# First product of blocks 3 to 6 with seven multiplications for eight, in a fused attention and feed-forward kernel

## The chip, the cores and the metric

The kernel runs on one core of one Trainium2 chip. The metric is device microseconds for one launch; lower is better. Three runs of the kernel before took 614.77, 615.26 and 616.49 us; the median is 615.26.

## The reference

Chunked attention with a few memory keys, and after it two matrix products with a gate between them:

```python
for c in range(nc):                          # 24 chunks of 32 queries, 4 x 8 heads of 64
    k_ctx = k[:, :, l_start:r_end]           # 16 keys to the left, 8 to the right
    k_full = np.concatenate([mem_k, k_ctx], axis=2)     # 8 memory keys ahead
    v_full = np.concatenate([mem_v, v_ctx], axis=2)
    scores = scale * np.matmul(q_c, k_full.transpose(0, 1, 3, 2))
    a = softmax(scores)
    out[:, :, c_start:c_end] = np.matmul(a, v_full)
x = out.transpose(0, 2, 1, 3).reshape(3072, 512)
h = x @ w_in                                 # 512 x 2048, the first product
g = np.where(h >= 1, h, np.where(h <= -1, 0.0, (h + 1) ** 2 / 4))
return g @ w_out                             # 2048 x 512, the second product
```

All of it is in float32.

## The kernel before, in words

The 3072 tokens are cut into six blocks of 512 (`TB`); the text counts them from 1, the code from 0. For each block, attention yields x transposed, with 512 features in four slices of 128 partitions (`NP`) by 512 tokens. The hidden width of 2048 is cut into 16 slices of 128 (`NFC`), and one slice of one block is a step.

Every float32 operand of the two products is split into two float32r parts, a high one (the rounded value) and a low one (the rest), and each product is made of three: high by high, high by low, low by high. `pe_hidden` (line 398) so has 12 matmuls a step, 4 slices of features by 3, with 128x128 weights as the stationary and 512 tokens as the moving operand, into one PSUM bank `ps_h`. `gating` (407) makes the gate on ScalarE from two Relus that read the bank and a Square; `gate_sum` (417) joins them on VectorE, `gate_high` (422) rounds on ScalarE to `gh`, and `gate_low` (428) subtracts on VectorE to `gl`. `pe_out` (433) has 12 matmuls of 512 columns, 4 groups of 128 tokens by 3, with gh and gl as stationary, accumulated over all 16 steps into four banks `ps_o`. A step is thus 24 matmuls of 512 columns, and `pe_out` follows two steps (`LAG`) after `pe_hidden`.

The weights come as 64-bit words, 16 tiles of 1 MB (`load_w`), and `decode` (153) turns each in place into high and low parts `wr`, with five VectorE and two ScalarE instructions, four of the seven on 128x1024 words. They stay in SBUF, so they are decoded while block 1 runs.

Blocks 1 and 2 are worked in half steps of 256 tokens (`half_step`, 452): 12 matmuls of 256 columns into `ps_h`, the gate on 256 columns, 6 matmuls of 512 columns. In the table `FIRST` (32) the letters A and B are the halves of block 1, C and D of block 2, w a decode, g attention of block 1, n0 to n3 the attention halves of blocks 2 and 3, and + the next load. A name stands once for each stage of its chain, and the table sets the order in which all engines get their instructions. From block 3 on, the loop at line 590 sets the order, a step at a time, with the attention of the next block begun at steps 3 and 9 (`STARTS`).

The attention of a half block (`attention`, 374, or the same calls in the loop) is `pe_scores` (64 matmuls of 64 columns, `ps_s`; the trace shows each float32 matmul of the attention twice), `less_max` (two VectorE instructions of 128x1024), an Exp on ScalarE, `normalise` (four on VectorE), `transpose_prob` (six VectorE transposes), `pe_values` (`ps_x`), `x_high` (two ScalarE copies out of PSUM) and `x_low` (two VectorE subtractions). Each half's qk and v tiles are loaded ahead from SyncE's queue, into one buffer each.

All engines' instructions are kept in program order (`InOrder`, 60), so no engine takes a later instruction while an earlier one waits. SyncE issues all loads and stores but the last half store. All these calls go through line 68, the line that the profile shows for them; the tiles' names tell them apart.

Of the kernel before, what the change touches and what calls it, by code (L numbers as in the profile page):

```python
# [27 lines left out]
FIRST = """
    + + g0 g0 g0 + g0 g1 g0 + g0 g0 g1 g1 g0 g1 + g1 g0 w0 g1 g1 + g1 g0 w0 g1 w0 + g0 g1 w0 w0 g2 +
    g0 w0 g1 w1 g2 + g2 g1 g0 g3 g2 + g1 g2 A0 + g3 g3 g2 g2 g3 g2 A1 A0 + g3 w2 g3 g3 g3 g2 w1 A1
    w1 + g2 g3 w3 w1 g2 g3 A0 w1 g3 w2 + w2 g2 g3 A0 g2 w4 g3 A0 B0 w1 + w2 A0 B0 A1 w2 B0 B1 w3 +
    B0 w2 A1 A2 B1 B0 A1 w3 A1 + A2 B1 w5 w3 B0 B1 A2 w3 + B1 B2 w4 A2 w3 w6 B1 A2 B2 + w4 A3 w7 B2
    w4 B2 A2 A3 + B2 w5 w4 B3 A3 w5 w8 B2 A3 w4 + B3 A4 w9 A3 B3 w5 B3 A3 + A4 B3 w6 w5 A4 B4 w6 A4
    w10 + A4 B3 w5 B4 A5 w11 w6 + B4 w6 A4 w7 w7 B4 A5 B5 B4 w12 + A5 w6 B4 A5 B5 A5 w7 w13 A6 + B5
    w7 w8 A5 w8 B5 A6 B6 B5 w14 A6 w7 A6 B5 B6 A6 w8 w15 A7 B6 w8 w9 A6 w9 B6 A7 B6 B7 A7 w8 A7 B6
    B7 A7 w9 A8 B7 w9 w10 w10 A7 B7 A8 B7 B8 A8 w9 A8 B7 A8 B8 w10 A9 B8 w10 w11 w11 B8 A8 A9 B8 A9  # L40
    B9 w10 A9 A9 B8 w11 B9 B9 A10 w11 w12 w12 B9 A9 A10 B9 w11 B10 A10 w12 A10 B9 B10 A10 w12 w13
    A11 B10 w13 B10 A10 A11 B10 w12 n0 A11 w13 A11 B11 + n0 w13 B10 A11 B11 n0 A12 B11 n0 w13 B11
    A11 A12 n0 B12 n0 n0 B11 n0 B11 B12 A12 n0 A12 A13 A12 n0 n0 A12 A13 w14 n0 B13 w14 n0 A14 B13
    n0 B12 n0 w14 B12 B12 w14 A13 w15 B12 A13 + w14 n0 A13 A14 B14 w15 A13 n0 n0 B14 B13 n1 w15 B13
    B13 w15 A15 A14 + n1 A14 B13 A15 A14 w15 B15 n1 A14 B14 n1 A15 B14 n1 C0 A15 B15 n1 n1 B14 n1
    B14 C0 A15 n1 A15 n1 n1 C1 n1 n1 C2 C1 B15 n1 B15 C0 B15 n1 C0 A15 C2 C0 C1 A15 C2 C1 C2 B15 C1
    + n1 C2 n1 n1 C0 B15 D0 B15 C1 D0 D0 D1 D0 D0 C3 D1 D1 C2 D1 C3 D1 D0 C3 C3 C3 D2 D1 D2 D2 D3 D2
    D2 C4 D3 D3 C3 D3 C4 D3 D2 C4 C4 C4 D4 D3 D4 D4 D5 D4 D4 C5 D5 D5 C4 D5 C5 D5 D4 C5 C5 C5 D6 D5
# [671 lines left out]
```

## Time and profile before

| | |
|---|---|
| Median of three runs | 615.26 us (614.77 to 616.49) |
| Span of the profiled execution | 613.5 us; its own time is not listed apart, and the median is 1.8 us above the span |
| TensorE matmul busy | 596.3 us, 97% |
| TensorE weight load busy | 500.1 us, 82% |
| VectorE busy | 331.1 us, 54% |
| ScalarE busy | 291.3 us, 47% |
| Mean granted TensorE clock | 0.983 |
| DMA | 55.36 MB, 90 GB/s over the span |

PE stands for TensorE's matmuls, PEld for its weight loads, DVE for VectorE, ACT for ScalarE, SP for SyncE. Matmuls are pipelined: the record of one reaches past the start of the next, so the distance from start to start is what one costs in a stream. A row of a group gives the instruction with what it writes and reads, the count, the busy time, the mean ns of one, and how long the engine had been idle before it. A row of the chain gives start, length, engine, the tile written and the count.

### The profile page before, as it was taken

How to read it: one execution, taken by the hardware profiler on the slowest of the kernel's cores; microseconds unless marked ns; L12 is line 12 of the kernel's file. 1: busy time of each engine (PE TensorE's matmuls, PEld its weight loads, DVE VectorE, ACT ScalarE, POOL GpSimd, SP SyncE). 2: the span in 40 equal slices, each digit the busy share in tenths (PEclk: the TensorE clock that was granted, in tenths of full speed). 3: DMA queues.
4: the chain of work that ended last, by engine and by line, in shares of the span. 5: the costliest groups of instructions: out<-in, count | busy, mean ns of one | idle time of the engine just before them, and what ended most of it. 6: DMA issues, size and time to landing. Idle time of an engine off the chain costs nothing.

```text
span 613.5 us, 12988 instructions
## 1 busy us (share of the span) xinstructions
PE 596.3 (97%) x5784; PEld 500.1 (82%) x5784; DVE 331.1 (54%) x514; ACT 291.3 (47%) x599; POOL 0.7 (0%) x6
## 2 busy tenths in 40 slices
PE   5899999999999999999999999999999999999997
PEld 2789998889988888888888888888888888888885
DVE  5899999983266734735523643732563732322222
ACT  2689865554444454434344344344443434433442
POOL 0000000000000000000000000000000000000000
PEclk7689999999999999999999999999999999999999
DMA  9999002322022222122201212100410000100001
GB/s 356 423 417 411 7 1 105 131 93 90 0 105 88 87 71 92 81 71 104 71 0 70 104 70 105 38 33 0 173 69 2 0 2 0 70 0 2 0 1 68
DMA packets 9992, 55.36 MB, mean 90 GB/s; under 512 B 1104, under 2 KB 1360, under 8 KB 5328
## 3 DMA queue, kind: packets, MB, share of 16 engines
q1 hardware_dynamic: 9792, 54.40, 23.1%
q8 instruction: 45, 0.74, 0.5%
q10 hardware_dynamic: 144, 0.13, 0.1%
q14 instruction: 11, 0.09, 0.1%
HBM read 48.23 MB, written 6.29 MB: 89 GB/s over the span
## 4 chain that ended last, share of the span: by engine, by line
PE 79%; DVE 16%; issue 2%; ACT 1%; DMA 1%
PE ps_h L68 37%; PE ps_o L68 37%; DVE f L68 5%; PE ps_x L68 3%; PE ps_s L68 2%; DVE wr L68 2%; DVE gw L68 2%; DVE pr L68 1%; DVE gl L68 1%; DVE pt L68 1%; DVE den L68 1%; DVE mx L68 1%; DMA qk<-in_first_qk_dram 1%; DVE xtl L68 1%; ACT pr L68 0%
## 5 line engine op out<-in xcount | busy, mean ns | idle before, releaser
L68 PE MATMUL ps_h<-xth,wr 128*128 128x256 f32 (+1 forms) x1024 | 273.3, 341 | 0.3 <-ACT xth L68 0.3
L68 PE MATMUL ps_o<-wr,gh 128*128 128x512 f32 x768 | 241.6, 396 | 0.0
L68 PEld LDWEIGHTS ps_h<-xth,wr 128*128 128x128 f32 x1024 | 180.9, 192 | 24.4 <-ACT xth L68 0.4
L68 PE MATMUL ps_h<-xtl,wr 128*128 128x256 f32 (+1 forms) x512 | 166.1, 340 | 1.0 <-DVE xtl L68 1.0
L68 PEld LDWEIGHTS ps_o<-wr,gh 128*128 128x128 f32 x768 | 141.7, 189 | 29.4
L68 DVE SCALAR_TENSOR_TENSOR gw<-gw,gt 128x256 f32<-128x256 f32 (+1 forms) x128 | 71.1, 557 | 168.3 <-ACT gw L68 167.5
L68 PE MATMUL ps_o<-wr,gl 128*128 128x512 f32 x384 | 151.6, 395 | 0.1
L68 ACT ACTIVATE gw<-ps_h 128x256 f32<-128x256 f32 (+1 forms) x128 | 62.6, 489 | 166.8 <-PE ps_h L68 165.8
L68 PEld LDWEIGHTS ps_h<-xtl,wr 128*128 128x128 f32 x512 | 98.2, 192 | 14.0 <-DVE xtl L68 1.6
L68 DVE TENSOR_TENSOR gl<-gw,gh 128x256 fp32r<-128x256 f32 (+1 forms) x128 | 70.8, 555 | 66.5 <-ACT gh L68 65.7
L68 ACT CAST gh<-gw 128x256 fp32r<-128x256 f32 (+1 forms) x128 | 65.5, 514 | 63.9 <-DVE gw L68 63.9
L68 PEld LDWEIGHTS ps_o<-wr,gl 128*128 128x128 f32 x384 | 72.4, 189 | 18.1 <-DVE gl L68 1.1
L68 ACT ACTIVATE gw<-gw 128x256 f32<-128x256 f32 (+1 forms) x128 | 67.3, 526 | 0.0
L68 ACT ACTIVATE gt<-ps_h 128x256 f32<-128x256 f32 (+1 forms) x128 | 62.2, 486 | 0.0
L68 DVE STREAM_TRANSPOSE pt<-pr 32x512 f32<-32x512 f32 (+1 forms) x60 | 41.2, 698 | 1.3
L68 DVE SCALAR_TENSOR_TENSOR f<-w,f 128x1024 uint32<-128x1024 uint32 x32 | 39.1, 1221 | 0.4
L68 ACT ACTIVATE pr<-pr 128x1024 f32<-128x1024 f32 (+1 forms) x14 | 13.1, 938 | 41.2 <-DVE pr L68 41.2
L68 PEld LDWEIGHTS ps_x<-pt,v 64*64 64x64 f32 x1536 | 25.6, 142 | 5.4 <-issue 3.4
L68 PE MATMUL ps_x<-pt,v 64*64 64x32 f32 x1536 | 27.4, 226 | 1.1 <-DVE pt L68 0.6
L68 ACT CAST xth<-ps_x 128x512 fp32r<-128x512 f32 x24 | 13.0, 594 | 24.8 <-PE ps_x L68 24.8
L68 PEld LDWEIGHTS ps_s<-qk 64*32 64x32 f32 x1536 | 16.9, 110 | 8.0 <-issue 4.6
L68 PE MATMUL ps_s<-qk 64*32 64x64 f32 x1536 | 19.5, 235 | 3.3 <-issue 1.4
(27 smaller groups left out, 179.3 us busy)
## 6 DMA issues: line engine op xcount, KB each, us to landing
w<-in_w_dram SPq DMA_DIRECT2D x16, 1024.0 KB, 19.7
qk<-in_qk_dram SPq DMA_DIRECT2D x10, 1536.0 KB, 6.5
v<-in_vw_dram SPq DMA_DIRECT2D x10, 1024.0 KB, 4.9
out_dram<-ob SPq DMA_DIRECT2D x23, 256.0 KB, 2.0
qk<-in_first_qk_dram SPq DMA_DIRECT2D x4, 768.0 KB, 8.7
v<-in_first_v_dram SPq DMA_DIRECT2D x4, 512.0 KB, 12.7
out_dram<-ob ACTq DMA_DIRECT2D x1, 128.0 KB, 2.3
out_dram<-ob SPq DMA_DIRECT2D x1, 128.0 KB, 2.5
```

Source lines behind the costliest of these rows:

```text
L68: return self.tc.keep_in_program_order(getattr(self.engine, name)(*args, **kwargs))
```

## The change

Blocks 3 to 6 make the first product in another way. Four slices of the hidden width form a quad, two pairs `s` of slices. For each pair the product of 512 features by 256 hidden columns with 512 tokens is cut in halves on all three sides, and made with Winograd's form of Strassen's scheme: seven products instead of eight, of sums of weights (four for each pair, in `build`) and of sums of x (`S1` to `S4`, in `SUMS`). A product has two times 6 matmuls of 256 columns (2 slices of features by 3), one half bank for each pair. The products add up in place in two banks, X and Y. Of h's four quarters, 11, 12 and 22 are made from a ScalarE copy of X (`copy_out`) to which VectorE adds Y (`add_up`); 21 is read in X. Gate, rounding and second product then go on as before, in groups of 12 second-product matmuls (`pe_out`), with the same number in all.

The sums of weights are made in block 2, in eight builds (the letter t in `FIRST`): two VectorE adds of a weight's high and low parts, four subtractions, one ScalarE cast to the high part, one VectorE subtraction for the low part, into the one buffer `st`, from which a 1 MB store goes to DRAM (`saved`). From there they are read back for each quad into holes, the places of weights in SBUF that blocks 3 to 6 no longer need: two loads of 256 KB after each of four products (`load_t`). Blocks 4 and 6 go through the quads in reverse, so that the quad at a turn is not loaded anew.

The attention of blocks 3 to 6 leaves x in plain float32 (`x_plain`, two ScalarE copies a half); `sum_up` (four VectorE instructions a block) and `split` (seven pairs of a ScalarE rounding and a VectorE subtraction) take the place of the four low parts. The order of blocks 3 to 6 is no longer set by a loop over steps but by the tables `QUADS`, one for each quad of a block: p is a product, c a copy out, a the adding up, r the Relus and Square, m the joining, h and l the high and low parts, g a group of second products, d a sum and k a split of x, 0 and 1 the next stage of an attention half of the next block, @S and @V its scores and values with the next loads, z a store; a leading minus means the quad before. x's tiles of blocks 1 and 2 have pools of their own, which are given up to the new tiles; gh and gl have four buffers instead of three, and the identity takes one of gl's until it is needed.

```diff
-LAG = 2
-STARTS = (3, 9)
+SECOND = 2
 FIRST = """
...
-    + n1 C2 n1 n1 C0 B15 D0 B15 C1 D0 D0 D1 D0 D0 C3 D1 D1 C2 D1 C3 D1 D0 C3 C3 C3 D2 D1 D2 D2 D3 D2
...
+    C1 + n1 C2 n1 n1 C0 B15 t0 C1 D0 B15 D0 t0 D0 D1 t0 D0 t0 C3 t0 C2 D0 D1 t0 t0 D1 t0 C3 t1 C3
...
+PROD = {
+    1: ("X", "A11", None),
+    2: ("Y", "A12", None),
+    6: ("X", "S2", 0),
+    5: ("Y", "S1", 1),
+    7: ("X", "S3", 2),
+    4: ("X", "A22", 3),
+    3: ("Y", "S4", None),
+}
+QUADS = (
...
+    p1 -h12 1 p2 c1 1 a11 r11 1 -l12 m11 -g21 -g22 p6 1 c2 p5 1 p7 c3 a22 h11 -g12 r22 m22 l11 1 p4
...
-    ident = const.tile([P, P], F32, name="ident")
+    ident = gpool.tile([P, P], F32, name="ident", tag="gl", bufs=4)
...
-        x_high(key)
-        yield
-        yield from x_low(key)
+        if key[0] < SECOND:
+            x_high(key)
+            yield
+            yield from x_low(key)
+        else:
+            x_plain(key)
+            yield
...
+    saved = dram.tile([NFC // 2, P, 4, 2, HQ], F32, name="saved")
+    def build(m):
...
+        fef = apool.tile([P, 2, 2, HQ], F32, name="fef", tag="f", bufs=2)
+        for j in range(2):
+            hi, lo = (weights(0, 2 * m + j, part).bitcast(F32) for part in range(2))
+            dve.tensor_tensor(fef[:, j].rearrange("p a b -> p (a b)"), hi, lo, op=ALU.add)
+            yield
+        b11, b21, b12, b22 = (fef[:, j, k] for j in range(2) for k in range(2))
+        tf = apool.tile([P, 4, HQ], F32, name="tf", tag="f", bufs=2)
+        dve.tensor_tensor(tf[:, 1], b12, b11, op=ALU.subtract)
+        yield
+        dve.tensor_tensor(tf[:, 2], b22, b12, op=ALU.subtract)
+        yield
+        dve.tensor_tensor(tf[:, 0], b22, tf[:, 1], op=ALU.subtract)
+        yield
+        dve.tensor_tensor(tf[:, 3], b21, tf[:, 0], op=ALU.subtract)
+        yield
+        st = ahead["y0"].tile([P, 4, 2, HQ], F32R, name="st", tag="st")
+        act.copy(st[:, :, 0], tf)
+        yield
+        dve.tensor_tensor(st[:, :, 1], tf, st[:, :, 0].bitcast(F32), op=ALU.subtract)
+        sp.dma_start(saved[m], st.bitcast(F32))
+        yield
+    def load_t(i, q):
+        for s in range(2):
+            sp.dma_start(hole(i, s).bitcast(F32), saved[2 * q + s, :, i])
...
+    def split(name):
+        k = side(name)
+        src = plain_of(name) if name != "S3" else plain["s"][:, 1]
+        act.copy(k[:, 0], src)
+        dve.tensor_tensor(k[:, 1], src, k[:, 0].bitcast(F32), op=ALU.subtract)
...
+    def product(i, q):
+        to, name, _ = PROD[i]
+        x = side(name)
+        for s in range(2):
+            terms = [(0, 0, cc) if lo == 0 else (0, 1, cc) for cc in range(2) for lo in range(2)]
+            terms += [(1, 0, cc) for cc in range(2)]
+            for n, (wp, xp, cc) in enumerate(terms):
+                pe.matmul(
+                    bank[to][:, s * HQ : (s + 1) * HQ],
+                    stationary(i, q, s, wp)[:, cc * P : (cc + 1) * P],
+                    x[:, xp, cc],
+                    start=i in (1, 2, 5) and s == 0 and n == 0,
...
+    def copy_out(n, key):
...
+        act.copy(t, bank["X"])
...
+    def add_up(name, key):
+        h = now.pop((*key, {"11": "c1", "22": "c3", "12": "c2"}[name]))
+        dve.tensor_tensor(h, h, bank["Y"], op=ALU.add)
...
+            elif what == "p":
+                i = int(which)
+                product(i, q)
+                if PROD[i][2] is not None and at + 1 < len(line) and line[at + 1][1] != q:
+                    load_t(PROD[i][2], line[at + 1][1])
```

Where the orders differ: first TensorE in the middle of block 3, before. `ps_h` with `xth` and `xtl` is a step's first product, `ps_o` with `gh` and `gl` the second; the numbers are those of the tiles.

```order
1516 L68 MATMUL ps_o_3946<-wr_12_1167,gh_4589 128x512 x2
1517 L68 MATMUL ps_o_3946<-wr_12_1167,gl_4590 128x512
1518 L68 MATMUL ps_o_3946<-wr_12_1167,gh_4589 128x512 x2
1519 L68 MATMUL ps_o_3946<-wr_12_1167,gl_4590 128x512
1520 L68 MATMUL ps_h_4665<-xth_3327,wr_13_1289 128x512 [waits Activation_49]
1521 L68 MATMUL ps_h_4665<-xtl_3328,wr_13_1289 128x512
```

And now, in the third quad of block 3: products 6, 5 and 7 (`s2`, `s1` and `s3` are the sums of x), `ps_h_3094` being bank X and `ps_h_3095` bank Y, with the waits for the read-back (DMAHW).

```order
1081 L94 MATMUL ps_h_3094<-s2_2962,wr_0_247 128x256 [waits DMAHW3_49,Activation_49]
1082 L94 MATMUL ps_h_3094<-s2_2962,wr_0_247 128x256 x5
1083 L94 MATMUL ps_h_3094<-s2_2962,wr_2_556 128x256 [waits DMAHW4_49]
1084 L94 MATMUL ps_h_3094<-s2_2962,wr_2_556 128x256 x5
1085 L94 MATMUL ps_h_3095<-s1_3085,wr_4_696 128x256 [waits DMAHW5_49,DVE_49]
1086 L94 MATMUL ps_h_3095<-s1_3085,wr_4_696 128x256 x5
1087 L94 MATMUL ps_h_3095<-s1_3085,wr_6_813 128x256 [waits DMAHW6_49]
1088 L94 MATMUL ps_h_3095<-s1_3085,wr_6_813 128x256 x5
1089 L94 MATMUL ps_h_3094<-s3_3088,wr_8_943 128x256 [waits DMAHW7_49,Activation_49]
1090 L94 MATMUL ps_h_3094<-s3_3088,wr_8_943 128x256 x5
```

In place of 12 wide matmuls into a bank of the step's own, 12 narrow ones each go to X, Y and X again, and row 1089 waits for ScalarE's copy of what 1081 to 1084 added up.

That copy on ScalarE, before (one step's gate and the rounding of the next):

```order
487 L68 ACTIVATE gw_5129<-ps_h_5116 128x512 [waits PE_49]
488 L68 ACTIVATE gt_5130<-ps_h_5116 128x512
489 L68 ACTIVATE gw_5129<-gw_5129 128x512 [waits Activation_49]
490 L68 CAST gh_5147<-gw_5129 128x512 [waits DVE_49]
491 L68 ACTIVATE gw_5164<-ps_h_5151 128x512 [waits PE_49]
```

And now, in the quad before the one above (`gt` and `u2` take the copies of X, `gh` is the rounding, `xp` the plain x of the next block's attention):

```order
350 L94 COPY gt_3390<-ps_h_3094 128x512 [waits PE_49]
351 L94 ACTIVATE gw_3409<-gt_3390 128x512 [waits DVE_49]
352 L94 ACTIVATE gt_3390<-gt_3390 128x512 [waits Activation_49]
353 L94 ACTIVATE gw_3409<-gw_3409 128x512
354 L94 COPY u2_3440<-ps_h_3094 128x512 [waits PE_49]
355 L94 CAST gh_3442<-gw_3409 128x512 [waits DVE_49]
356 L94 COPY gt_3542<-ps_h_3094 128x512 [waits PE_49]
357 L94 ACTIVATE gw_3545<-gt_3542 128x512 [waits DVE_49]
```

The gate no longer reads the bank but a copy to which VectorE has added Y, and the second copy (354) stands behind the three gating operations of the first (351 to 353).

Last VectorE early in block 2, before: only the joining (`gw`) and the low part (`gl`) of half steps.

```order
205 L68 SCALAR_TENSOR_TENSOR gw_2020<-gw_2020,gt_2021 128x256 [waits Activation_49]
206 L68 TENSOR_TENSOR gl_2023<-gw_2020,gh_2022 128x256 [waits PE_49,Activation_49]
207 L68 SCALAR_TENSOR_TENSOR gw_2020<-gw_2020,gt_2021 128x256 [waits Activation_49]
208 L68 TENSOR_TENSOR gl_2023<-gw_2020,gh_2022 128x256 [waits Activation_49]
209 L68 SCALAR_TENSOR_TENSOR gw_2088<-gw_2088,gt_2089 128x256 [waits Activation_49]
```

And now, with the second build (`fef` the whole weights, `tf` their sums, `st` the parts to be stored):

```order
205 L94 TENSOR_TENSOR fef_1964<-wr_1_477 128x512
206 L94 SCALAR_TENSOR_TENSOR gw_1948<-gw_1948,gt_1949 128x256 [waits Activation_49]
207 L94 TENSOR_TENSOR fef_1964<-wr_2_556 128x512
208 L94 TENSOR_TENSOR tf_1990<-fef_1964 128x256 [waits DVE_49]
209 L94 TENSOR_TENSOR tf_1990<-fef_1964 128x256
210 L94 TENSOR_TENSOR gl_1951<-gw_1948,gh_1950 128x256 [waits Activation_49]
211 L94 TENSOR_TENSOR gl_1951<-gw_1948,gh_1950 128x256
212 L94 SCALAR_TENSOR_TENSOR gw_2008<-gw_2008,gt_2009 128x256 [waits Activation_49]
213 L94 TENSOR_TENSOR tf_1990<-fef_1964,tf_1990 128x256 [waits DVE_49] x2
214 L94 TENSOR_TENSOR fef_2021<-wr_3_625 128x512 [waits DVE_49]
215 L94 TENSOR_TENSOR gl_2011<-gw_2008,gh_2010 128x256 [waits Activation_49]
216 L94 TENSOR_TENSOR st_2019<-tf_1990,st_2019 128x4x256 [waits DMAHW2_49,Activation_49]
```

Between the gating of half steps stand the builds' instructions, each ahead of gating that comes later in the order.

More of the change, by code (lines that the diff above doesn't have):

```diff
@@ L179, in x_of @@
         if blk not in xts:
[L180 removed]
+            xts[blk] = [xpools[blk].tile([P, NP, TB], F32R, name=n) for n in ("xth", "xtl")]
         return xts[blk]
@@ new lines, in attn_ffn_kernel, with pe_out @@
+    HOUT = {"11": (0, 0), "12": (1, 0), "21": (0, 1), "22": (1, 1)}
+    begun = set()
+    def pe_out(blk, q, name, pieces=None):
+        odd, half = HOUT[name]
+        gh, gl = now[blk, q, name, "g"]
+        if blk not in acc:
+            acc[blk] = [None] * NT
+        if acc[blk][2 * half] is None:
+            pair = two_banks(f"a{half}", "ps_o")
+            acc[blk][2 * half : 2 * half + 2] = [pair[:, t] for t in range(2)]
+        for s, t in pieces or ((0, 0), (0, 1), (1, 0), (1, 1)):
+            fc = 2 * (2 * q + s) + odd
+            wh, wl = weights(1, fc, 0), weights(1, fc, 1)
+            ts = slice(s * HQ + t * P, s * HQ + (t + 1) * P)
+            to = (blk, 2 * half + t)
+            for i, (g, w) in enumerate(((gh, wh), (gh, wl), (gl, wh))):
+                pe.matmul(
+                    acc[blk][2 * half + t], g[:, ts], w, start=to not in begun, stop=True, skip_group_check=True
+                )
+                begun.add(to)
@@ new lines, in attn_ffn_kernel, with small @@
+    order = {}
+    for blk in range(SECOND, NB):
+        order[blk] = list(range(NQ))[:: 1 if blk % 2 == 0 else -1]
+    line = [(blk, q) for blk in range(SECOND, NB) for q in order[blk]]
+    def small(shape, name, tag, bufs, dtype=F32):
+        return gpool.tile(shape, dtype, name=name, tag=tag, bufs=bufs)
+    def copy_out(n, key):
+        if n == 2:
+            t = small([P, TB], "u2", "u2", 1)
+        else:
+            t = small([P, TB], "gt", "gt", 2)
+        act.copy(t, bank["X"])
+        now[(*key, f"c{n}")] = t
@@ new lines, in left, with left_store, finish @@
+    def left(which):
+        two = {"22": (0, 2), "21": (2, 4), "12": (4, 4)}[which]
+        for blk, half, fc in items[len(items) - LAST :][slice(*two)]:
+            next(chains[f"{'ABCD'[2 * blk + half]}{fc}"], None)
+    def left_store(half):
+        for _ in chains["CD"[half] + str(NFC - 1)]:
+            pass
+    def finish():
+        key = line[-1]
+        high("12", key)
+        low("12", key)
+        for t in range(2):
+            pe_out(*key, "22", ((0, t), (1, t)))
+            pe_out(*key, "21", ((0, t), (1, t)))
+            last_store(2 + t)
+        for t in range(2):
+            pe_out(*key, "12", ((0, t), (1, t)))
+            last_store(t)
+        let_go("y0")
+        let_go("y1")
```

387 lines of the change are left out of this document (232 added, 155 removed).

## The prediction

> **What bounds the kernel now.** I read the busy times first, then the slices of the span, then the chain that ended last in order of time, then TensorE's waits.
>
> ```profile
> PE 596.3 (97%) x5784; PEld 500.1 (82%) x5784; DVE 331.1 (54%) x514; ACT 291.3 (47%) x599; POOL 0.7 (0%) x6
> ...
> PE   5899999999999999999999999999999999999997
> ...
> DVE  5899999983266734735523643732563732322222
> ACT  2689865554444454434344344344443434433442
> ```
>
> TensorE is busy in every slice but the first, second and last. VectorE is full only up to about 125 us (the eighth slice ends at 123 us), where the weights are decoded; after that it stands between 2 and 7 tenths. So what happens to TensorE's own work decides, unless new waits appear. The chain in order of time gives TensorE's pace, first in block 2 (half steps, 256 columns a matmul), then in blocks 3 to 6 (full steps, 512 columns):
>
> ```profile
> 155.35 1.43 PE ps_h L68 x12
> 156.79 1.39 PE ps_o L68 x6
> 158.17 2.87 PE ps_h L68 x24
> 161.05 2.77 PE ps_o L68 x12
> ...
> 241.89 1.41 PE ps_s L68 x91
> ...
> 536.80 2.76 PE ps_h L68 x12
> 539.56 2.80 PE ps_o L68 x12
> ...
> 597.89 2.76 PE ps_h L68 x12
> 600.65 8.38 PE ps_o L68 x36
> ```
>
> From 536.80 to 597.89 lie 11 full steps: 61.09 / 11 = 5.554 us for 24 matmuls, 0.2314 us each. In block 2, 24 matmuls of 256 columns take 2.87 us, 0.1196 us each. That is a little more than half of 0.2314 (0.1157), so a narrow matmul pays about 4 ns of its own. Before the steady part, TensorE hardly waits, even while VectorE is full:
>
> ```profile
> PE ps_x L68 <- DVE pt L68: 0.6, 2, 0.4
> PE ps_h L68 <- DVE xtl L68: 0.5, 1, 0.5
> PE ps_s L68 <- issue: 0.4, 1, 0.4
> ```
>
> These are all of TensorE's waits between 60 and 250 us, 1.5 us together. The profiled span is 613.5 us. The runs have a median of 615.26, which leaves 1.8 us around the span; I add these at the end.
>
> **The products.** Before, four steps held 4 x 12 matmuls of 512 columns for the first product and as many for the second: 4 x 5.554 = 22.22 us. A quad replaces them. Its first product has 7 products x 12 matmuls of 256 columns, 84 x 0.1196 = 10.05 us, and its second product is unchanged, 48 x 0.2314 = 11.11 us, together 21.16. That is 1.06 us less a quad. There are 16 quads: **17.0 us less TensorE work**, all of it on the path. If second-product matmuls are priced at 2.80 for 12, as they stand beside 512-column work, the gain is 16 x (4 x 2.76 - 10.05) = 15.8; if at 2.77, as they stand beside 256-column work, 16 x (22.22 - 10.05 - 11.08) = 17.4. I keep 15.8 to 17.4 as its bounds and take 17.0, the pace averaged over both kinds. One eighth of the first product would have been 22 us (16 x 11.04 / 8); the rest goes to the narrower matmuls.
>
> Narrower matmuls also mean 336 weight loads a block for 192, and a row shows what a load takes by itself:
>
> ```profile
> L68 PEld LDWEIGHTS ps_h<-xth,wr 128*128 128x128 f32 x1024 | 180.9, 192 | 24.4 <-ACT xth L68 0.4 <-issue 0.2
> ```
>
> A load's record is 192 ns long, yet the 256-column matmuls of block 2 follow each other at 120 ns, so there the loads run beside the matmuls. [...]
>
> **The sums of weights in block 2.** Each of 8 builds gives VectorE two adds of 128x512, four subtractions of 128x256 and one of 128x1024, and ScalarE one cast of 128x1024. The durations, then how densely such instructions can follow each other, then the stage:
>
> ```profile
> L68 DVE SCALAR_TENSOR_TENSOR gw<-gw,gt 128x512 f32<-128x512 f32 x64 | 44.2, 691 | 138.2 <-ACT gw L68 137.8
> L68 DVE SCALAR_TENSOR_TENSOR gw<-gw,gt 128x256 f32<-128x256 f32 x64 | 26.8, 422 | 30.1 <-ACT gw L68 29.7
> L68 DVE TENSOR_TENSOR wr<-f,wr 128x1024 fp32r<-128x1024 f32 x16 | 19.5, 1220 | 1.2 <-ACT wr L68 1.2
> L68 ACT CAST wr<-f 128x1024 fp32r<-128x1024 f32 x16 | 16.8, 1053 | 5.9 <-DVE f L68 5.8
> ```
>
> ```profile
> 60.94 0.42 DVE L68 SCALAR_TENSOR_TENSOR gw<-gw,gt 128x256 f32<-128x256 f32 x1
> 61.27 1.22 DVE L68 TENSOR_TENSOR wr<-f,wr 128x1024 fp32r<-128x1024 f32 x1
> 62.41 0.42 DVE L68 TENSOR_TENSOR gl<-gw,gh 128x256 fp32r<-128x256 f32 x1
> ...
> 112.78 0.69 DVE L68 TENSOR_SCALAR f<-w 128x1024 uint32<-128x1024 uint32 x1
> 113.38 1.22 DVE L68 TENSOR_TENSOR wr<-f,wr 128x1024 fp32r<-128x1024 f32 x1
> ```
>
> ```profile
> 80.00:120.00 40.00, 39.24 (x605) 35.33 (x604) 39.40 (x61) 23.41 (x57) 0.00 (x0) 1.00 0.20 69
> ...
> 138.20:190.80 52.60, 52.53 (x455) 47.37 (x455) 24.84 (x50) 25.57 (x74) 0.00 (x0) 1.00 0.15 56
> 190.80:223.80 33.00, 33.00 (x561) 29.84 (x561) 19.10 (x36) 15.91 (x44) 0.00 (x0) 1.00 0.33 114
> ```
>
> By durations a build is 2 x 0.691 + 4 x 0.422 + 1.220 = 4.29 us, eight 34.3. By spacing, when each follows an independent one (0.60, 0.33 and 1.14 us), it is 3.66, eight 29.3. By the order they stand between the first half steps of block 2 and the values of block 3's first attention half, which is 138.2 to 190.8 in the trace before: VectorE (third busy time of the row) is busy 24.8 of 52.6 there and idle 27.8. So VectorE lacks 1.5 to 6.5 us, less what its own gating saves when packed: some 36 of the 50 instructions are 128x256, which packed take 0.33 for 0.42, 3 us less. What is lacking at the end of the stretch is -1.5 to 6.5 us, and TensorE waits for that unless it can run on ahead. It has room: gh and gl have four buffers of two half steps each, and from 190.8 to 223.8 VectorE has 13.9 us idle. The row of 80 to 120 us is the nearest: there VectorE was busy 39.4 of 40 us and TensorE 39.2, with the waits above. I take **1.0 us lost**, bounds -0.5 (those waits vanishing) and 6.5. ScalarE gains 8 x 1.05 = 8.4 us in a stretch where it was busy 25.6 of 52.6; that hides.
>
> The one buffer st makes a cast wait until the store before it has landed. The issue rows price such transfers:
>
> ```profile
> qk<-in_qk_dram SPq DMA_DIRECT2D x10, 1536.0 KB, 6.5
> v<-in_vw_dram SPq DMA_DIRECT2D x10, 1024.0 KB, 4.9
> out_dram<-ob SPq DMA_DIRECT2D x23, 256.0 KB, 2.0
> ```
>
> A store of 1 MB should then take about 4.9 us, and between one build's last subtraction and the next cast stand about 4 us of VectorE work, so ScalarE may wait up to 1 us a build. Behind that cast stand the gating operations of the next half step; they reach TensorE only when the room above is used up. It is within the 1.0.
>
> **The read-backs.** A load of a hole is 256 KB, 2.0 us by the last row (a store; as a load, between 2.0 and 4.9). Its issue waits on SyncE's queue for the product that last read the hole, and its reader comes one quad later less one product, 19 us or more. Queued behind it are the other holes, the qk and v loads and the stores; even behind a qk and a v load (11.4 us) it is in time. The first quad's eight loads follow the v load that waits for the values of block 3's second half, and before their first reader TensorE has five half first products and three half second ones of block 2 (5 x 1.43 + 3 x 1.39), scores (1.41), two products and 12 second-product matmuls (2.87 + 2.78): 18 us for 3 MB of holes and v, which at the rate of the qk row take 13. Cost nothing; without that cover a quad would wait some 2 us, 16 quads 32 us.
>
> **Two banks for seven products.** Every product adds into bank X or Y in place, so TensorE must wait until a bank has been copied or added out. The handoff by the trace:
>
> ```profile
> 599.57 1.08 PE L68 MATMUL ps_h<-xth,wr 128*128 128x512 f32 x4
> 600.48 0.64 PE L68 MATMUL ps_o<-wr,gh 128*128 128x512 f32 x2
> 600.68 0.60 ACT L68 ACTIVATE gw<-ps_h 128x512 f32<-128x512 f32 x1 [2.57 <-PE ps_h L68]
> ```
>
> ScalarE starts 0.20 us after TensorE has gone on to its next work, and 0.60 later the bank is read; with 0.05 for the signal, 0.85. Where only one product on the other bank lies between (product 6, then 5, then 7 back on X), the cover is 12 x 0.1196 = 1.43, 0.58 to spare. That needs ScalarE to be free when product 6 ends. Ahead of that copy in its queue (rows 351 to 353 of the order) stand the three gating operations of output 11, which wait for VectorE's add:
>
> ```profile
> L68 ACT ACTIVATE gw<-gw 128x512 f32<-128x512 f32 x64 | 40.4, 632 | 0.0
> L68 ACT CAST gh<-gw 128x512 fp32r<-128x512 f32 x64 | 39.8, 622 | 41.7 <-DVE gw L68 41.7
> L68 DVE TENSOR_TENSOR xtl<-ps_x,xth 128x512 fp32r<-128x512 f32 x24 | 15.4, 682 | 7.0 <-ACT xth L68 7.0
> ```
>
> In the second and third quad of a block, products 1 and 2, then two groups of 12 second-product matmuls (5.55) and product 6 (1.43) lie ahead of it. From the end of product 2 the add is done by 0.20 + 0.68 + 0.05 and, with a low part and an attention step queued before it, about 3 us, the gating by 5; product 6 ends at 7.0. That is 2 us clear. In the first quad of a block only one such group lies there, but another stands between products 5 and 7; in the last, a group and attention values stand between 6 and 7. The other handoffs have a group of 2.77 or more between. More work on the engines per block: ScalarE 12 copies of 0.60 and 7 splits of 0.62, 11.5 us, VectorE 12 adds and 7 sums and splits net (11 new, 4 former low parts gone) at 0.69, 13.1 us, of 85 us each; from 4 and 5 tenths they go to about 6 and 7. I take **0.5 us lost** for the four blocks, the turn from block 2 and the end together, bounds 0 and the rival below. The end itself has the same form: 36 second-product matmuls (8.38), then half-width copies and two stores.
>
> **The sum.** 613.5 - 17.0 + 1.0 + 0.5 = 598.0 us of span, with 1.8 around it 599.8 us.
>
> **The rivals.** *VectorE binds in block 2.* If packing saves nothing and TensorE cannot run ahead, 6.5 us come back: 613.5 - 17.0 + 6.5 + 0.5 + 1.8 = 605.3, still faster. For it: the stretch would be full; against it: 80 to 120 us.
> *The bank handoff binds (slower).* If in each quad one copy finds the three gating operations just started, the bank is free at 0.20 + 3 x 0.632 + 0.60 + 0.05 = 2.75 us, 1.32 beyond the cover; 16 quads lose 21.1: 613.5 - 17.0 + 21.1 + 1.8 = 619.4. It decides from 1.06 us a quad. For it: both queues grow fuller and hold their order, so one late add delays the copy behind it. Against: the 2 us clear.
> *Weight loads bind.* If each product matmul cost its load's 192 ns, a quad would be 16.1 + 11.1 = 27.2, 5 us longer, 80 us in all, 695. The 2.87 for 24 speaks against it.
> *Nothing is won.* That would need 48 x 0.2314 / 84 = 0.132 us a narrow matmul, or four fifths of the handoff rival's wait: 615.3. The order shows 84 narrow matmuls a quad for 48 wide, so the change does what it says.
>
> **How the numbers follow.** Forecast near 599.8: 0.74. VectorE in block 2: 0.13. Handoff: 0.08, weight loads 0.01, nothing won 0.04. A measurement of this kernel can tell about 0.3%, 1.8 us, from no change. Faster 0.74 + 0.13 = 0.87, same 0.04, slower 0.09. The range goes from 613.5 - 17.4 - 0.5 + 1.8 = 597.4 to the block 2 rival with the smaller gain, 605.3 + 1.2 = 606.5; it leaves out the last three.
>
> **What would show it.** In the chain afterwards, ps_h pieces of 12 matmuls at 1.43 us with quads of about 21.2 us, waits of TensorE in blocks 3 to 6 under 1 us together, and VectorE near full from 138 to 191 us with TensorE full beside it. Wrong: TensorE waiting for a ScalarE copy of ps_h once a quad, for a read-back of wr, or for gl in block 2; or narrow matmuls at another pitch than 0.120.

## The result and the profile after

The changed kernel takes 610.08 us (median of five runs, 609.2 to 610.63) beside 615.48 us (five runs, 614.77 to 619.5) for the kernel before on the same chip. The ratio is 0.9897, with an interval of 0.9873 to 0.9922 (the quotient of the two medians is 0.991). It is faster by about 1%, a little over a third of what was forecast (5.4 us by the medians, where the forecast of 599.8 us had 15.5), and it lies above the range. The profiled execution took 609.82 us with a span of 608.0, so 1.8 us lie around the span, as before.

The page's busy times and slices answer to the first fence of the prediction:

```profile
PE 583.4 (96%) x6360; PEld 518.6 (85%) x6360; DVE 402.0 (66%) x643; ACT 344.8 (57%) x683; POOL 0.7 (0%) x6
...
PE   5799999999996999999999999999999999999996
...
DVE  5799999997899575755557655556655557423332
```

One slice of TensorE stands out, the thirteenth (182 to 198 us) with 6 tenths. Every slice behind it but the last is full. The chain in order of time, in block 3, shows the pace there:

```profile
257.69 5.57 PE ps_o L94 x24
263.26 4.28 PE ps_h L94 x36
```

36 narrow matmuls take 4.28 us, 0.119 each, and 24 wide ones 5.57, 0.232 each. The windows by stage say that TensorE waits for nothing from 230 us to the tail (the second number is TensorE's busy time; one of four such rows):

```profile
320.00:405.00 85.00, 85.00 (x993) 75.97 (x993) 51.11 (x77) 47.72 (x83) 0.00 (x0) 1.00 0.45 137
```

What a block gained can be read from the start of one half's scores in one block to the same in the next. First the kernel before, then the changed one, from the timeline of TensorE:

```profile
241.82 0.39 PE L68 MATMUL ps_s<-qk 64*32 64x64 f32 x23
...
338.27 0.96 PE L68 MATMUL ps_s<-qk 64*32 64x64 f32 x73
```

```profile
324.35 0.86 PE L94 MATMUL ps_s<-qk 64*32 64x64 f32 x66
...
416.62 1.11 PE L94 MATMUL ps_s<-qk 64*32 64x64 f32 x91
```

96.45 us became 92.27, 4.18 a block, 16.7 us for four blocks. The gain was made. It was given back in three places. The largest is block 2: TensorE's waits between 60 and 250 us were 1.5 us together before, and now are

```profile
PE ps_h L94 <- ACT gt L94: 5.2, 2, 5.0
PE ps_s L94 <- issue: 1.2, 2, 0.8
PE ps_x L94 <- DVE pt L94: 0.8, 3, 0.3
PE ps_o L94 <- issue: 0.5, 1, 0.5
```

One wait of 5.0 us makes most of it. The timeline of ScalarE, VectorE and TensorE around it shows who is late for whom:

```profile
186.37 1.04 ACT L94 CAST st<-tf 128x1024 fp32r<-128x1024 f32 x1 [4.33 <-DMA saved<-st]
187.32 0.38 ACT L94 ACTIVATE gw<-ps_h 128x256 f32<-128x256 f32 x1
...
181.16 1.22 DVE L94 TENSOR_TENSOR st<-tf,st 128x1024 fp32r<-128x1024 f32 x1
...
185.44 0.42 DVE L94 TENSOR_TENSOR tf<-fef,tf 128x256 f32<-128x256 f32 x1
...
188.02 0.58 PE L94 MATMUL ps_h<-xth,wr 128*128 128x256 f32 x1 [4.97 <-ACT gt L94]
188.40 0.41 PE L94 MATMUL ps_h<-xtl,wr 128*128 128x256 f32 x1
188.62 0.41 PE L94 MATMUL ps_h<-xth,wr 128*128 128x256 f32 x1
...
190.75 0.80 PE L94 MATMUL ps_o<-wr,gh 128*128 128x512 f32 x2
```

ScalarE stands before the cast of the seventh build. Behind that cast in its queue are the Relus that empty the two ps_h banks, and TensorE has nowhere to put the next half step. The cast could start only when two things were done. The build's last sum on VectorE ended at 185.86 (the row at 185.44). The store of the build before, which began after VectorE's split at 181.16 + 1.22, landed just ahead of the cast's start at 186.37. The profile puts the wait to the DMA, since it came last, but VectorE was only half a microsecond ahead of it; and there VectorE is full (third busy number, now and before, same ten microseconds). Before, it had 1.2 us to spare in them:

```profile
180.00:190.00 10.00, 5.03 (x29) 4.42 (x29) 10.00 (x19) 4.80 (x11) 0.00 (x0) 0.88 0.29 119
```

```profile
180.00:190.00 10.00, 10.00 (x66) 9.09 (x66) 8.83 (x18) 5.36 (x16) 0.00 (x0) 1.00 0.05 20
```

After the wait the narrow matmuls follow each other at about 0.212 us (188.40, 188.62) in place of 0.120. The granted clock (the number after the five busy times) is 0.50 there:

```profile
188.00:190.70 2.70, 2.68 (x12) 2.68 (x13) 2.70 (x5) 1.13 (x4) 0.00 (x0) 0.50 0.41 167
```

The twelve of this half step take 2.73 us, from 188.02 to the next group at 190.75, in place of 1.43: another 1.3 us.

The second place is the tail, where two matmuls into one bank wait for the copy of the other bank of the same tile:

```profile
597.13 0.73 PE L94 MATMUL ps_o<-wr,gh 128*128 128x512 f32 x2 [0.78 <-DVE ob L94]
602.37 0.73 PE L94 MATMUL ps_o<-wr,gh 128*128 128x512 f32 x2 [0.78 <-DVE ob L94]
```

The third is at the start. First before, then now:

```profile
22.11 1.06 PE L68 MATMUL ps_s<-qk 64*32 64x64 f32 x51 [1.05 <-issue]
```

```profile
22.82 1.06 PE L94 MATMUL ps_s<-qk 64*32 64x64 f32 x51 [1.68 <-issue]
```

In the traces of the experiments the same gap is between 0.93 and 1.89 us. So these 0.6 us vary from one execution to the next, and one trace of the kernel before can't show whether any of them are the change's.

Together: 613.5 - 16.7 + 7.6 in block 2 (6.8 of waits between 138 and 240 us, where there were 0.5 before, and 1.3 for the slow half step) + 2 in the tail (1.6 of waits; from the matmul before each to the one after it 1.18 us, 595.95 to 597.13 and 601.19 to 602.37, where a stream has 0.23) + 0.6 at the start = 607.0, against a span of 608.0. The last 1.0 us is not accounted for.

### The profile page after: what moved, and what is told of

The parts are those of the page before. It is cut to its first block, busy times and chain, and to the rows that moved or that the text cites. A ratio compares the mean times of both kernels' runs of the same rounds, so it can differ in the third digit from the quotient of the medians.

```text
span 608.0 us, 14641 instructions
## 1 busy us (share of the span) xinstructions
PE 583.4 (96%) x6360; PEld 518.6 (85%) x6360; DVE 402.0 (66%) x643; ACT 344.8 (57%) x683; POOL 0.7 (0%) x6
## 4 chain that ended last, share of the span: by engine, by line
PE 74%; DVE 20%; issue 2%; ACT 2%; DMA 1%; DVEq 0%
PE ps_o L94 36%; PE ps_h L94 32%; DVE f L94 5%; PE ps_x L94 3%; PE ps_s L94 2%; DVE pt L94 2%; DVE wr L94 2%; DVE gw L94 2%; DVE pr L94 2%; DVE gl L94 2%; DVE den L94 1%; DVE st L94 1%; DVE mx L94 1%; DVE tf L94 1%; DMA qk<-in_first_qk_dram 1%
## 5 line engine op out<-in xcount | busy, mean ns | idle before, releaser
L94 PE MATMUL ps_h<-xth,wr 128*128 128x256 f32 x512 | 104.4, 291 | 5.5 <-ACT gt L94 5.2
L94 PE MATMUL ps_h<-s,wr 128*128 128x256 f32 x768 | 98.1, 282 | 0.0
L94 PEld LDWEIGHTS ps_h<-s,wr 128*128 128x128 f32 x768 | 95.5, 188 | 1.9
L94 PEld LDWEIGHTS ps_h<-xth,wr 128*128 128x128 f32 x512 | 85.3, 195 | 8.5 <-ACT gt L94 5.8
L94 PE MATMUL ps_h<-xtl,wr 128*128 128x256 f32 x256 | 66.3, 289 | 0.6 <-DVE xtl L94 0.6
L94 DVE TENSOR_TENSOR gt<-gt,ps_h 128x512 f32<-128x512 f32 x32 | 21.9, 686 | 53.9 <-ACT gt L94 43.2
L94 PEld LDWEIGHTS ps_h<-xtl,wr 128*128 128x128 f32 x256 | 50.2, 196 | 2.5 <-DVE xtl L94 0.8
L94 ACT ACTIVATE gw<-ps_h 128x256 f32<-128x256 f32 (+1 forms) x80 | 34.1, 426 | 31.5 <-PE ps_h L94 29.4
L94 PEld LDWEIGHTS ps_h<-sa,wr 128*128 128x128 f32 x384 | 47.9, 188 | 1.4
L94 PE MATMUL ps_h<-sa,wr 128*128 128x256 f32 x384 | 48.8, 282 | 0.0
```

Of the source, the lines that this page charges most:

```text
L94: return self.tc.keep_in_program_order(getattr(self.engine, name)(*args, **kwargs))
```

## The experiments

Three theories for the wait near 183 us: the *store* (one buffer st, so a cast waits until the store before it has landed), the *order* (the Relus stand behind the cast on ScalarE), and *VectorE* (too much work in too short a time). Each kernel was run four to seven times. The ratios are to the kernel before, run on the same chip (615.45 to 615.72 us).

### Two buffers for st

```diff
-            ahead["y0"] = hold("y0", "right")
+            ahead["z0"] = hold("z0", "right")
...
-        st = ahead["y0"].tile([P, 4, 2, HQ], F32R, name="st", tag="st")
+        st = ahead["z0"].tile([P, 4, 2, HQ], F32R, name="st", tag="st", bufs=2)
...
             if 0 not in plain:
+                let_go("z0")
+                ahead["y0"] = hold("y0", "right")
```

> The builds' parts get two st buffers in turn instead of one, nothing else. In the profile of the change ScalarE stood 4.33 us before the seventh build's cast, put down to the store of the sixth; TensorE stood 4.97 us behind it. Store theory (the one buffer's store is the cause): both waits go, and with them the slow matmuls after them, 610.1 - 5 to 6 = about 604.5. VectorE theory (the sums that the cast reads were ready only 0.5 us before the store had landed): the cast starts 0.5 us earlier, 609.6.

Measured: 609.35 us, ratio 0.9897 (0.9883 to 0.9911). The ratio is that of the changed kernel, so nothing clear was gained. TensorE still waits 4.5 us for ScalarE's gt. ScalarE's wait now carries another name:

```profile
183.81 1.05 ACT L94 CAST st<-tf 128x1024 fp32r<-128x1024 f32 x1 [3.93 <-DVE tf L94]
```

The store is not the sole cause. With it out of the way, VectorE's sum is what the cast waits for, and the wait is 0.4 us shorter, as the timeline above would have it.

### The Relus ahead of the cast

```diff
-    t5 t5 C7 D8 t5 n2 n2 D7 t6 n2 t5 C7 D8 n2 D8 C7 t5 t6 n2 t6 t6 t6 C8 n2 D9 D8 t6 n2 t7 t6 n2 t6
-    C7 + n2 t7 C8 n2 t7 D9 C9 D8 n2 t7 n2 C8 C8 t7 D9 t7 n2 D9 t7 C8 C6 t7 n2 D10 C9 D9 D10 + C9 C8
+    t5 t5 C7 D8 t5 n2 n2 D7 t6 n2 t5 C7 D8 n2 D8 C7 t5 t6 n2 t6 t6 t6 C8 n2 D9 D8 t6 n2 t7 C8 D9 t6 n2 t6
+    C7 + n2 t7 n2 t7 C9 D8 n2 t7 n2 C8 C8 t7 D9 t7 n2 D9 t7 C8 C6 t7 n2 D10 C9 D9 D10 + C9 C8
```

> In the table of blocks 1 and 2 the gating operations of the half steps C8 and D9 stand ahead of the seventh build's cast instead of behind it; the work is the same. Order theory (TensorE waited because ScalarE takes its queue in order and the late cast stood ahead of the operations that free a bank): the wait of 4.97 us and the slow matmuls behind it go, about 604. Capacity theory (VectorE has more to do in this stretch than there is time): the wait comes back within the next half steps, at gl or at the attention's values, 608 to 610.

Measured: 610.91 us, ratio 0.9922 (0.9907 to 0.9937). The wait came back one stage later, for the rounded gate in place of the Relus:

```profile
192.65 0.41 ACT L94 CAST gh<-gw 128x256 fp32r<-128x256 f32 x1 [5.94 <-DVE gw L94]
...
193.10 1.22 PE L94 MATMUL ps_o<-wr,gh 128*128 128x512 f32 x2 [4.21 <-ACT gh L94]
```

The Relus were made in time, but VectorE, busy 10.00 of 10 us from 180 to 190, was late with the join of the gate (gw). The order on ScalarE alone is not the cause. TensorE's waits between 138 and 240 us came to 5.6 us, less than the 6.8 of the changed kernel, and yet the time is no shorter: the granted clock behind the wait was 0.65 in the mean of 190 to 200 us and 0.84 in 200 to 210, where the changed kernel had 0.94 and 1.00.

### One build for eight

Seven of the eight builds and their stores are left out, and every read-back takes the first build's sums.

```diff
+        if m > 0:
+            yield
+            return
...
-            sp.dma_start(hole(i, s).bitcast(F32), saved[2 * q + s, :, i])
+            sp.dma_start(hole(i, s).bitcast(F32), saved[0, :, i])
```

> Seven of the eight builds are left out, and all read-backs read the first one's sums, so outputs of blocks 3 to 6 are wrong; reads, products and blocks 3 to 6 are as before. If block 2's loss is the builds' doing, by whatever way, the 9 us by which block 2 took longer than in the kernel before go: about 601. If it has another source (pools, loads, order): 606 to 610.

Measured: 602.63 us, ratio 0.9786 (0.9774 to 0.9799). Block 4's first scores, in the changed kernel and here:

```profile
234.78 1.48 PE L94 MATMUL ps_s<-qk 64*32 64x64 f32 x128
```

```profile
227.83 1.48 PE L94 MATMUL ps_s<-qk 64*32 64x64 f32 x128
```

Seven of the eight builds cost 7.4 us by the medians and 7.0 by these rows. The read-backs are all still made here, and no wait of TensorE is put to them.

### The last outputs in banks of different tiles

```diff
         if acc[blk][2 * half] is None:
...
+            if blk == NB - 1:
+                if "last" not in ahead:
+                    ahead["last"] = two_banks("s", "ps_o")
+                acc[blk][2 * half + 1] = ahead["last"][:, half]
```

> In the last block the two token groups of each half are added up in banks of different tiles, so that the copy of one does not hold back the matmuls of the other. Bank theory (the two waits of 0.78 us for a copy near the end, with their restarts, are the tile's doing): 610.1 - 1.6 to 2.2 = about 608.2. If the end waits for the copies and stores anyway: 610.1.

Measured: 608.18 us, ratio 0.9879 (0.9864 to 0.9893), 1.9 us below the changed kernel. The two waits for ob are gone, and the second product's matmuls run without a gap from 590 us to the end. So the tail costs about 2 us; the pairs of runs below narrow it down.

### The softmax later

The letters n2 are the attention of block 3's first half, t6 and t7 the last two builds.

```diff
-    t5 t5 C7 D8 t5 n2 n2 D7 t6 n2 t5 C7 D8 n2 D8 C7 t5 t6 n2 t6 t6 t6 C8 n2 D9 D8 t6 n2 t7 t6 n2 t6
-    C7 + n2 t7 C8 n2 t7 D9 C9 D8 n2 t7 n2 C8 C8 t7 D9 t7 n2 D9 t7 C8 C6 t7 n2 D10 C9 D9 D10 + C9 C8
...
+    C7 D8 t5 D7 t6 t5 C7 D8 D8 C7 t5 t6 t6 t6 t6 C8 D9 D8 t6 t7 n2 n2 t6 t6 C7 t7 C8 n2 t7 D9 C9 n2
+    D8 t7 C8 C8 t7 n2 D9 t7 n2 D9 n2 t7 C8 n2 C6 + t7 n2 D10 n2 C9 D9 n2 D10 n2 C9 n2 C8 C9 n2 D10
...
```

> The softmax, transposes and values of block 3's first half (VectorE's rows of 0.69 to 1.22 us, some 10 us in all) stand about 16 steps of the order by hand later, behind the last build's sums instead of between those of builds 6 to 8; nothing else is moved and no work is taken away. Capacity theory (VectorE had more to do between 180 and 197 us than the time there holds): the 4.97 us wait of TensorE near 183 us shrinks below 1 us, VectorE's 200 to 210 us (5.28 of 10 busy in the changed kernel) take the work up, the time is 605 to 607 us. Rival, the builds cost as much wherever VectorE's other work stands (the chain of sum, cast and split inside a build sets the pace): within 1 us of the changed kernel's 610.1 us. Rival, the attention now comes too late and the wait returns ahead of block 3's first products near 235 us: 609 to 612 us, with a wait of TensorE on sa or s there.

Measured: 610.45 us, ratio 0.9909 (0.9881 to 0.9937). That is what the rivals gave, and it looked like the end of the theory of VectorE: TensorE waits 5.28 us in the same place. But here too the wait changed its name:

```profile
185.67 1.05 ACT L94 CAST st<-tf 128x1024 fp32r<-128x1024 f32 x1 [6.02 <-DMA saved<-st]
```

VectorE's last sum of the seventh build now ended at 183.3, and the store of the sixth build landed at 185.6. Two causes of nearly one size stood side by side, each hiding behind the other. Two buffers took the store away and VectorE stayed; the later softmax relieved VectorE and the store stayed.

### The first sums on GpSimd

```diff
-            dve.tensor_tensor(fef[:, j].rearrange("p a b -> p (a b)"), hi, lo, op=ALU.add)
+            pool.tensor_tensor(fef[:, j].rearrange("p a b -> p (a b)"), hi, lo, op=ALU.add)
```

> The first step of each build, the sum of the two copies of each slice (16 instructions of 0.681 us on VectorE, 10.9 us), is made by GpSimd, which is idle in block 2; the order is the same. Capacity theory: VectorE's 10.00 of 10 busy us in 180 to 190 fall by some 2 us and the wait near 183 us by at least as much, since the backlog there has built up over builds 6 to 8: 604 to 607 us. Rival, GpSimd is slow at this (no row of it in the trace) or slows VectorE's own rows while it runs: the builds' subtractions wait for it, rows of tf take over 0.45 us, and the time is 609 to 614 us.

Measured: 612.76 us, ratio 0.9945 (0.9922 to 0.9968), slower than the changed kernel, as the rival had it. The groups of this kernel, GpSimd's and some of VectorE's between 138 and 236 us; then the first two of VectorE's in the changed kernel:

```profile
L94 POOL TENSOR_TENSOR fef<-wr 128x512 f32<-128x512 f32 x16 | 23.7, 1505 | 165.8 <-DMA out_dram<-ob 137.6 <-DVE tf L94 28.2
...
L94 DVE SCALAR_TENSOR_TENSOR gw<-gw,gt 128x256 f32<-128x256 f32 x27 | 14.4, 539 | 6.9 <-ACT gw L94 6.7
L94 DVE TENSOR_TENSOR st<-tf,st 128x1024 fp32r<-128x1024 f32 x8 | 13.3, 1660 | 3.2 <-ACT st L94 3.2
...
L94 DVE TENSOR_TENSOR tf<-fef,tf 128x256 f32<-128x256 f32 x16 | 6.7, 417 | 0.1
```

```profile
L94 DVE SCALAR_TENSOR_TENSOR gw<-gw,gt 128x256 f32<-128x256 f32 x29 | 12.1, 422 | 5.3 <-ACT gw L94 5.0
L94 DVE TENSOR_TENSOR st<-tf,st 128x1024 fp32r<-128x1024 f32 x8 | 9.8, 1223 | 2.5 <-ACT st L94 2.4
```

GpSimd's row has 1.505 us for what VectorE does in 0.681, and VectorE's own joins go from 0.422 to 0.539 us and its splits from 1.223 to 1.660. What was taken off VectorE came back in part as longer instructions. They are not those that the rival named: tf stayed at 0.42 us. Joins and splits read two tiles in SBUF. What made them longer is not shown. Single instructions of the softmax in this run also differ by what they read (ps_s lies in PSUM, the other tiles in SBUF):

```profile
178.96 2.53 POOL L94 TENSOR_TENSOR fef<-wr 128x512 f32<-128x512 f32 x2 [3.58 <-DVE tf L94]
187.40 3.48 POOL L94 TENSOR_TENSOR fef<-wr 128x512 f32<-128x512 f32 x2 [5.90 <-DVE tf L94]
...
179.99 1.23 DVE L94 TENSOR_TENSOR pr<-ps_s,mx 128x1024 f32<-128x1024 f32 x1
187.45 2.29 DVE L94 TENSOR_TENSOR pr<-pr,rin 128x1024 f32<-128x1024 f32 x1
215.69 1.23 DVE L94 TENSOR_TENSOR pr<-pr,rin 128x1024 f32<-128x1024 f32 x1
```

Beside GpSimd's adds, the one with an input in PSUM took 1.23 us, and the one with two in SBUF 2.29, where its fellow at 215.69, with GpSimd idle, took 1.23.

### Either mend with the new tail

The edits are those of the runs above, two at a time.

> The later softmax together with the last block's outputs in banks of different tiles, which by itself gave 608.18 against 610.08 us. If the two mends are of different places they add up: the time of the later softmax alone less 1.9 us, 603 to 605 us. If not, no less than 1 us better than the better of the two.

Measured: 608.88 us, ratio 0.9875 (0.9847 to 0.9902), 1.6 us below the later softmax alone. The 603 to 605 us counted on a gain from the later softmax that did not come.

> GpSimd's sums together with the last block's outputs in banks of different tiles. If both hold: the time of the GpSimd run less 1.9 us, 602 to 605 us; if GpSimd is too slow: 607 to 612 us.

Measured: 610.46 us, ratio 0.9907 (0.9884 to 0.9931), 2.3 us below GpSimd alone. With the pair of the last section, the new tail is worth 1.6 to 2.3 us in four pairs, whatever block 2 costs, so it is a place of its own.

### Later softmax and two buffers at once

> The later softmax and two buffers for st at once. Theory of two limits of nearly one size: with one buffer the seventh build's cast waits for the store of the sixth (with the later softmax 6.02 us, put to the DMA saved<-st), and with the softmax in its old place it waits for the build's own last sum on VectorE (with two buffers 3.93 us, put to VectorE's tf); each mend by itself left TensorE a wait of 4.5 to 5.3 us, both together leave it under 1 us, and the time is 604 to 606 us. Rival, neither is the limit (ScalarE's queue with the narrow cast behind a build's sums makes the wait in any case): the wait stays at 4 us or more and the time at 609 to 611 us.

Measured: 609.0 us, ratio 0.9894 (0.987 to 0.9918). Half of the expectation held: the wait at 183 us fell from 5.28 to 1.66 us, so the two causes were there. But the time did not follow. The cast, and TensorE's waits between 138 and 240 us:

```profile
182.52 1.05 ACT L94 CAST st<-tf 128x1024 fp32r<-128x1024 f32 x1 [3.72 <-DVE tf L94]
```

```profile
PE ps_h L94 <- ACT gt L94: 1.7, 1, 1.7
PE ps_s L94 <- ACT xp L94: 1.2, 1, 1.2
PE ps_x L94 <- DVE pt L94: 1.2, 2, 0.7
PE ps_s L94 <- issue: 1.1, 1, 1.1
PE ps_o L94 <- DVE gl L94: 0.5, 1, 0.5
```

One long wait became six short ones, 5.7 us together where the changed kernel has 6.8. VectorE's busy time, which was 10.00 and 8.33 us in these two stretches, now is

```profile
180.00:190.00 10.00, 8.34 (x137) 7.11 (x124) 9.93 (x19) 4.17 (x9) 0.00 (x0) 1.00 0.66 237
190.00:200.00 10.00, 8.34 (x165) 6.84 (x163) 8.75 (x17) 3.51 (x9) 0.00 (x0) 1.00 0.57 239
```

The softmax had been moved by some 5.5 us only (its first instruction from 177.57 to 183.12 us), still among the builds, and the shortage moved with it. And the granted clock fell behind these waits too. Here is the stretch of 200 to 210 us, first in this run, then in the run with the builds moved, below; the changed kernel has 1.00 there:

```profile
200.00:210.00 10.00, 7.69 (x158) 6.34 (x152) 6.64 (x11) 5.93 (x14) 0.00 (x0) 0.66 0.72 254
```

```profile
200.00:210.00 10.00, 9.24 (x66) 8.34 (x65) 8.21 (x15) 3.68 (x10) 0.00 (x0) 1.00 0.72 264
```

By an estimate from the granted clock that is up to 3.4 us of TensorE's pace (10 us at 0.66; the half step at 0.50 in the changed kernel lost 1.3 of its 2.73 us), where the changed kernel lost up to 1.8 by the same estimate (0.88 in 180 to 190 us, 0.94 in 190 to 200). So the clock can have taken back the 1.1 us that the shorter waits had won.

### All three mends

> The later softmax, two buffers for st and the last block's outputs in banks of different tiles; the scores of block 3's second half stand four steps later too, since with the later softmax they waited 1.2 us for a bank. By the theory of two limits: the time of the run with the first two mends, less 1.9 us for the tail and about 1 us for the scores, 601 to 604 us, which is nearly that of the kernel with one build of eight less those 1.9 us (600.7). By the rival: 606 to 608 us.

Measured: 606.7 us, ratio 0.9846 (0.9825 to 0.9867), 2.3 us below the run before it: the tail, and a little of the scores' wait. The rival's number came true, and that of the theory did not. So the last form of the theory: it is the work between about 150 and 200 us that is too much, and only work moved out of that stretch helps.

### The last two builds moved out

The letters t6 and t7 stand at later half steps (some of the lines are shown), and the last two n2, the splits of the sides that take over the memory of st, stand at the end.

```diff
-    C11 D12 C10 n3 n3 C11 C12 n3 n3 D12 C12 D12 n3 n3 D12 + C11 n3 D13 n3 C11 D11 D13 C11 n3 D12 n3
...
+    C8 D9 n2 D9 C8 C6 n2 D10 C9 t6 D9 D10 + t6 C9 C8 n2 n2 t6 C9 D10 t6 C9 t6 C10 D11 t6 D9 D10 t6
...
+    D12 C12 D12 n3 n3 D12 + C11 n3 D13 n3 C11 D11 D13 t7 C11 n3 D12 n3 t7 C12 D12 C12 D13 t7 D13 D13
...
```

> The same work in block 2, one buffer for st: build 7 stands some 40 steps of the order by hand later (between the attentions of block 3's halves, where the changed kernel's VectorE was idle 4.5 us of 200 to 210) and build 8 some 100 later (behind the second attention, idle 7 us of 221 to 236); the splits of block 3's first sides, which share the memory of st, stand behind build 8. Capacity theory in its last form (VectorE's work of builds, gating steps and softmax between 150 and 200 us comes to about the time there, so a wait taken away at one place returns at the next; only moving work out of that stretch helps): TensorE's waits between 150 and 215 us come to under 2 us together, against 7 in the changed kernel and 5.6 with the later softmax and two buffers, VectorE's busy share falls to about 0.88 in 180 to 200 us, and the time is 604 to 606.5 us. Rival, the pace is set inside a build, wherever it stands (sum, cast, split and store one after another, with TensorE's relus queued behind the cast on ScalarE): waits of 4 us or more return beside builds 7 and 8, 608.5 us or more. A late split of block 3's first side would show as a wait of TensorE on sa near 232 us.

Measured: 603.71 us (603.29 to 606.62), ratio 0.9804 (0.9773 to 0.9835). That is a little better than was expected. With the whole of the work done, the time is 1.1 us from that with one build. Windows of 138 to 190 us, the changed kernel first:

```profile
138.00:190.00 52.00, 46.84 (x416) 42.28 (x415) 45.03 (x90) 28.17 (x71) 0.00 (x0) 0.98 0.39 154
```

```profile
138.00:190.00 52.00, 51.48 (x449) 46.52 (x447) 44.29 (x88) 28.63 (x75) 0.00 (x0) 1.00 0.46 180
...
200.00:236.00 36.00, 34.25 (x457) 30.55 (x456) 27.10 (x51) 18.92 (x49) 0.00 (x0) 1.00 0.63 214
```

TensorE has 51.48 of 52 us where it had 46.84, VectorE hardly less than before (44.29 for 45.03), and the work moved stands in 200 to 236, where VectorE's 22.6 us became 27.1. Block 4's first scores start 6 us earlier than in the changed kernel (234.78):

```profile
228.81 1.48 PE L94 MATMUL ps_s<-qk 64*32 64x64 f32 x128
```

TensorE's waits between 150 and 215 us come to 1.7 us, none over 0.8, and the granted clock is 1.00 from 138 to 240 us. The two builds are as dense as before: in the table build 7 reaches over 25 places for 24, build 8 over 26 for 28. ScalarE still stands 2.64 us for a store ahead of the sixth build's cast, and TensorE has no wait behind it until 189.94 us. So the rival, a pace set inside a build wherever it stands, did not come. Not shown is how much of the gain is VectorE's time, how much the store's and how much the clock's, since the move takes away the waits of all three.

### Spread builds with the new tail

> The spread builds and the last block's outputs in banks of different tiles: the time of the spread builds alone, less 1.9 us; by the capacity theory 602 to 604.5 us, below the 606.7 us of the three mends together.

Measured: 601.98 us (601.03 to 602.84), ratio 0.9767 (0.9736 to 0.9798). This is the fastest of all the kernels run: 13.5 us below the kernel before, 8.1 below the change as it was made.

## Why the forecast was too low

**The products, 17.0 us: right.** 4.18 us a block by the scores, 16.7 us in all. The narrow matmuls kept their 0.119 to 0.120 us, and TensorE has no wait between 230 us and the tail.

**The read-backs, nothing: right.** No wait of TensorE is put to wr<-saved.

**The bank handoff in the quads: right.** The rival that would have made the kernel slower did not come; no wait of TensorE is put to a copy or an add of a bank between 230 us and the tail. The 0.05 us for the signal has no row beside it in the prediction; in the profile after, the Relu that gt is made by ends at 187.97 us (187.59 + 0.38), and the matmul that waited for it starts at 188.02.

**The rivals.** Of the four, VectorE binding in block 2 (605.3 us) is the nearest to what came, but its cause was narrower (ten microseconds, not the stretch), its size larger, and the tail came on top of it. Weight loads did not bind, as the pace shows (0.119 us a matmul, beside loads recorded at 0.188 in the profile after).

**The end, within 0.5 us: too small.** The prediction gave the tail the form that it had before and priced it at nothing of its own. It costs 1.6 to 2.3 us (four pairs of runs): with two banks in one tile, matmuls into one waited for the copy of the other (0.78 us, twice), and with separate tiles no wait of TensorE is put to ob.

**The sums in block 2, "1.0 us lost, bounds -0.5 and 6.5": the step that failed.** It lost 7.6 us by the trace, and leaving out seven of the builds won 7.4 (the run with one). That is beyond the bound that the prediction itself had for it. That its upper bound, VectorE short of time over the whole stretch, came near is luck: VectorE was idle for 7 of the 52 us from 138 to 190, and it was not near full there, as the prediction gave for a sign. What failed is the cover, in three sentences.
- "It has room: gh and gl have four buffers". TensorE did not stop at gh and gl but at the two ps_h banks, a step earlier: they are emptied by Relus that stand on ScalarE behind a build's cast. The run with the Relus first then showed the gate itself late (4.2 us for gh, 1.2 for gl). Neither room covered the wait.
- "The row of 80 to 120 us is the nearest". In that stretch VectorE and TensorE are both full, which shows that such an order exists, not that this one is it. Here the whole stretch of 138 to 190 us has VectorE at 45.0 of 52, so on the mean it had time; but 138 to 180 us have 35.0 of 42, and the last ten 10.00 of 10, since the builds and the first softmax of block 3 stand there together. The trace before could have told it: in 180 to 190 us VectorE already had 8.83 of 10, so the 27.8 us of idle time that the prediction counted lay almost all elsewhere. The later idle time (from 190.8 to 223.8) was real, but this order did not use it; the order with the last two builds moved did, and got 6.4 us back.
- "ScalarE may wait up to 1 us a build" for the store, "within the 1.0". ScalarE stood 4.33 us at one build. The store by itself was within the price, 0.5 us later than VectorE's last sum; the sum, which the same cast waits for, was left out of it. Since both ended within 0.5 us of each other, each looked like the cause when the other was taken away.

A term that the prediction did not have at all is the granted clock: behind the wait of 5 us it was 0.50, and the half step there took 1.3 us more.

With the last two builds moved, seven builds cost about 1 us (228.81 for 227.83 at block 4's first scores), near what was forecast for all eight, and with the tail mended too the kernel stands at 602.0 us, inside the range. So the mechanism of the gain was right, and what the prediction took for granted was an order of the builds that this change did not have.

What stays open: the last 2 us between 602.0 and 599.8. TensorE's waits between 138 and 240 us are 2.9 us in the trace of the last kernel (0.5 before), and the start's gap is 1.78 us (1.05 before); neither was followed up.

## What to carry to other kernels

When work goes to an engine with idle time, look for the ten microseconds in which it must be done, not for the mean of a stage, and follow each buffer between the engines to the one that fills first. When a wait is mended and the time stays, read the name of the wait again before dropping the theory: a second cause of the same size may have stood behind the first, and what moves a shortage by a few microseconds doesn't end it. Moving the whole of the work to where the engine is idle was worth more here than every local mend.
